# Attention and two gated projections on one core: the transfers of SP's and GpSimd's queues take the list's order

## The chip, the core and the metric

The kernel runs on 1 core of one Trainium2 chip. Times are device microseconds of one execution. Where several executions were timed, their median stands with the lowest and the highest. One further execution was taken with the hardware profiler; all rows below are from that one.

## What is computed

Inputs are q, k, v of 4 batches, 8 heads, 576 positions, 64 values a head. The reference, cut to what matters (the attention has a coarse part on means of four positions and a banded part; two gated blocks follow):

```python
q_d = q.reshape(B, H, Sd, factor, D).mean(axis=3)          # k_d, v_d likewise; factor = 4
out_up = np.repeat(sm_attn(q_d, k_d, v_d), factor, axis=2)
mask = np.abs(pos[:, None] - pos[None, :]) < factor
scores = np.where(mask, scale * np.matmul(q, k.transpose(0, 1, 3, 2)), -1e9)
out_local = np.matmul(softmax(scores), v)
x = (out_up + out_local).transpose(0, 2, 1, 3).reshape(B, S, H * D)
h = np.maximum(x @ w_in, 0.0)                               # 512 -> 1024
x = (h * sigmoid(conv3(h))) @ w_out                         # 1024 -> 512
out = (sigmoid(causal_conv5(x)) * (x @ w_val)) @ w_out2     # 512 -> 512
```

The weights arrive as 64-bit floats and are made into 32-bit ones on the chip.

## The kernel before

**Steps.** Attention runs in 16 steps: step s is batch s // 4 and a pair of heads. A step transposes K and Q on PE (tpk, tpq), evacuates them on ScalarE (kT, qT), forms banded scores in blocks of 24 queries by 32 keys (sl) and coarse scores (sd), and multiplies the exponentials with V: avl and avm read the V windows of the step (a tile `ldw`), avd reads the sums of four V rows (a tile `vd`, or `vs` from step 4 on). The blocks a0, a1, ... are the products with w_in (tile `pa`, two blocks a group of 128 columns), b0, b1, ... those with w_out (`pb`), cc and d those of the second gated block (`pc`, `pd`).

**Loads.** On SP's queue: Lk and Lq (`load`, two transfers each from step 4 on) fetch K and Q of a step; Lw (`load_vw`) fetches the V windows of a step in twelve small transfers; Ls (`Weights.load`) fetches one of 16 weight stages of 512 KB, 0 to 7 of w_in and 8 to 15 of w_out; Lz and O are late weights and stores. On GpSimd's queue: Qv (`sum_v`) sums V rows for two steps with four transfers into one tile, of which the last three add to what is there and so wait for the one before; Ql (the last piece of `Weights.pieces`) adds a stage into the low half of the weights, `win` or `wout`.

**A weight job n.** Ls brings it, ab (ScalarE) and cv (VectorE) make 32-bit floats, hi and lo (ScalarE) write the high part and its negative, Ql adds the value to the latter. Four tags of stage buffers are used in turn, so that ab10 uses the place that job 2 leaves when Ql2 has landed. Block a(2f) and a(2f+1) need Ql f; b blocks of column group e need Ql(8 + 2e) and Ql(9 + 2e). p0 (ScalarE, first tap of the second convolution) writes a tile in the place of stages 3, 7, 11 and 14, and so waits for Ql14.

**What sets the order.** A list, `ORDER` (lines 852 to 917), names every operation. The loop at its end runs them in that order, each inside `ordered(F[name], ALL)`: whatever the operation issues on an engine of `ALL` is put behind the last instruction recorded for that engine. Recorded are the instructions that go through `mm` (PE) or a `Noted` object (`vec`, `act`, `pool`). Before, the list binds PE, VectorE and ScalarE:

```python
        with ExitStack() as st:
            for e in engines:
                if e in last:
                    st.enter_context(tc.issue_after(last[e].ins))
            fn()
...
    ALL = ("pe", "vec", "act")
```

The transfers of both queues are called as `nc.sync.dma_start` and `nc.gpsimd.dma_start`, are not recorded, and their place on their queue is the one that the scheduler finds, which may be ahead of the operations beside them in the list.

Of the kernel before, what the change touches and what calls it, by code (L numbers as in the profile page):

```python
# [45 lines left out]
def kernel(  # L46
# [13 lines left out]
    nc = tc.nc  # L60
# [21 lines left out]
    PW = 512  # L82
# [79 lines left out]
    class Weights:  # L162
# [3 lines left out]
            self.jobs = jobs  # L166
            self.stage = stage

        def load(self, n, queue=nc.sync):
            dst, src, r0, nr, c0 = self.jobs[n]  # L170
            wide = PW // nr
            rows = src[r0 * 128 : (r0 + nr) * 128]
            t, w = self.stage(n)
            if src.dtype == F32:
                queue.dma_start(
                    out=w.rearrange("p (r n) -> p r n", r=nr),
                    in_=rows.rearrange("(r p) n -> p r n", p=128)[:, :, c0 : c0 + wide],
                )
            else:
                queue.dma_start(  # L180
                    out=t.rearrange("p (r n) -> p r n", r=nr),
                    in_=rows.bitcast(I32).rearrange("(r p) n -> p r n", p=128)[
                        :, :, 2 * c0 : 2 * (c0 + wide)
                    ],
                )

        def pieces(self, n):
            dst, src, r0, nr, c0 = self.jobs[n]
            plain = src.dtype == F32
            t, w = self.stage(n)  # L190

            def to():
                return [d[:, c0 // 128, r0 : r0 + nr].rearrange("p r n -> p (r n)") for d in dst]

            words = t.rearrange("p (n t) -> p n t", t=2)
            return (
                lambda: plain or sign_off(act, w, words),
                lambda: plain or to_f32(vec, w, words),
                lambda: act.activation(out=to()[0], in_=w, func=AF.Copy),
                lambda: act.activation(out=to()[1], in_=to()[0].bitcast(F32), func=AF.Copy, scale=-1.0),  # L200
                lambda: nc.gpsimd.dma_start(out=to()[1].bitcast(F32), in_=w, accum_op=ALU.add),
            )

    actx = ExitStack()
# [6 lines left out]
    def load(src, tag, b, hp):  # L211

        if b == 0:
            slot = f"hg{'hi' if tag == 'ldk' else 'lo'}{hp}"
            if hp < 2:
                t = mp.tile([QT, 2, NT, D], F32, tag=slot, name=tag)
                nc.sync.dma_start(
                    out=t.rearrange("p e t d -> p e (t d)"),
                    in_=src[b, 2 * hp : 2 * hp + 2].rearrange("h (p t) d -> p h (t d)", p=QT),
                )  # L220
            else:
                t = mp.tile([QT, NT, 2, D], F32, tag=slot, name=tag)
                for e in range(2):
                    nc.sync.dma_start(  # L224
                        out=t[:, :, e, :], in_=src[b, 2 * hp + e].rearrange("(p t) d -> p t d", p=QT)
                    )
        else:
            t = ap.tile([QT, NT, 2, D], F32, tag=tag, name=tag, bufs=1)
            for e in range(2):
                nc.sync.dma_start(  # L230
                    out=t[:, :, e, :], in_=src[b, 2 * hp + e].rearrange("(t p) d -> p t d", p=QT)
                )
        T[tag, b, hp] = t

    def sum_v(s):

        b, hp = where(s)
        t = ap.tile([HD, 2, 2, 2, D], F32, tag="vs", name="vs")
        rows = v[b, 2 * hp : 2 * hp + 4].rearrange("h (s p r) d -> p (h s) r d", s=2, r=4)
        for r in range(4):  # L240
            nc.gpsimd.dma_start(  # L241
                out=t.rearrange("p t h s d -> p (t h s) d"),
                in_=rows[:, :, r],
                **({"accum_op": ALU.add} if r else {}),
            )
        for i in range(2):
            T["vd", s + i] = t[:, i]

    def load_v_first(part):

        if part == 0:
            first["v"] = keep.tile([HD, H, 2, 4, D], F32, tag="wout1", name="ldv")
        n = H // 2
        t = first["v"][:, part * n : part * n + n]
        nc.sync.dma_start(
            out=t.rearrange("p h s r d -> p (h s) (r d)"),
            in_=v[0, part * n : part * n + n].rearrange("h (s p r) d -> p (h s) (r d)", s=2, r=4),
        )
        for hp in range(part * HP // 2, (part + 1) * HP // 2):
            T["ldv", 0, hp] = first["v"][:, 2 * hp : 2 * hp + 2]  # L260
# [20 lines left out]
    def load_vw(b, hp):  # L281
        vw = ap.tile([128, NG, 2, D], F32, tag="ldw", name="ldw", bufs=1)
        for c in range(4):
            j = c * NG
            while j < (c + 1) * NG:
                n = 1 if j in (0, NB - 1) else min((c + 1) * NG, NB - 1) - j
                g = j - c * NG
                for e in range(2):
                    nc.sync.dma_start(
                        out=vw[KB * c : KB * c + KB, g : g + n, e],  # L290
                        in_=windows(b, 2 * hp + e, key_start(j), n),
                    )
                j += n
        T["ldw", b, hp] = vw
# [257 lines left out]
    E = {}  # L552
# [100 lines left out]
    def late_load(i):  # L653
        if "ep" not in E:
            actx.close()
            end_open()
        src, j = LATE[i]
        rows = src[j * 128 : j * 128 + 128]
        raw = E["ep"].tile([128, 2 * PW], I32, tag="stage", name="stage", bufs=3)
        if src.dtype == F32:  # L660
            nc.sync.dma_start(out=raw[:, :PW], in_=rows.bitcast(I32))
        else:
            nc.sync.dma_start(out=raw, in_=rows.bitcast(I32))
        E["raw", i] = raw

    def late_sign(i):
# [99 lines left out]
        act.activation(out=E["o", i], in_=E["pd", i], func=AF.Copy, scale=0.5)  # L766

    def store(i):
        nc.sync.dma_start(out=oflat[i * 128 : i * 128 + 128, :], in_=E["o", i])

    make_identity(nc, ident)
    for hp in range(3):
        load(k, "ldk", 0, hp)
        load(q, "ldq", 0, hp)
    load_v_first(0)
    load_vw_first(nc.sync, (0, 1, 2))
    pool.memset(mask, 0.0)
    m3 = mask[:, : NG * KB].rearrange("p (g k) -> p g k", k=KB)
    spans = [(c, 0, NG, 4) for c in range(4)]
# [275 lines left out]
```

## Time and profile before

| | us |
|---|---|
| three timed executions, median (lowest to highest) | 481.89 (480.61 to 482.44) |
| the profiled execution, own time | 479.92 |
| its span, first to last instruction | 478.0 |
| PE busy in the span | 427.8 (89%) |
| VectorE busy | 347.5 (73%) |
| ScalarE busy | 282.9 (59%) |
| GpSimd busy | 54.2 (11%) |

The span is cut into stretches below, because the engine that sets the pace differs between them. A busy PE is not PE at its peak: ends of matmuls are modelled. A line of a timeline starts with the time from the span's start and the duration; what stands in brackets at its end is the idle time of the engine just before it and what ended that.

### The profile page before, as it was taken

To read this page: it belongs to the slowest core of one execution; us is meant where nothing else is said; L and a number is where in the kernel's file an instruction comes from. 1 tells how busy PE (TensorE), PEld (TensorE's weight loads), DVE (VectorE), ACT (ScalarE), POOL (GpSimd) and SP (SyncE) were. 2 spreads that over 40 slices of the span, in tenths; PEclk is the share of its full clock that TensorE was granted. 3 is DMA by queue.
4 is the path that set the end of the run, shared out by engine and by line. 5 is a ranking of instruction groups with operands and counts; after the bars stand their busy time and mean duration, and the time that the engine had idled before them with its cause. 6 is when DMAs were issued, how large, how long until landed. Compare 5 with 4: busy or idle time off the path is not lost.

```text
span 478.0 us, 13683 instructions
## 1 busy us (share of the span) xinstructions
PE 427.8 (89%) x5873; PEld 396.6 (83%) x5873; DVE 347.5 (73%) x575; ACT 282.9 (59%) x628; POOL 54.2 (11%) x72
## 2 busy tenths in 40 slices
PE   6257078879999799999999999999999999999996
PEld 5236057779999798999999999999999998989985
DVE  3355099898998589998568769789999999932300
ACT  2344198787986386888657668555793554532221
POOL 8213012111222210022120000000000000000000
PEclk9755555679999899999999999999999999999999
DMA  9999568765466952144671211333000001011022
GB/s 188 169 192 224 132 124 212 187 140 134 94 91 129 122 86 52 36 85 54 108 109 32 63 32 34 134 98 124 1 1 0 2 1 66 23 67 45 22 89 88
DMA packets 90102, 42.91 MB, mean 90 GB/s; under 512 B 74198, under 2 KB 84354, under 8 KB 90042
## 3 DMA queue, kind: packets, MB, share of 16 engines
q1 hardware_dynamic: 73050, 33.88, 28.5%
q0 software_dynamic: 16992, 8.16, 13.5%
q8 instruction: 46, 0.75, 0.7%
q14 instruction: 14, 0.11, 0.1%
HBM read 33.08 MB, written 4.72 MB: 79 GB/s over the span
## 4 chain that ended last, share of the span: by engine, by line
PE 63%; DVE 16%; DMA 8%; SPq 7%; issue 4%; ACT 2%; POOL 1%; POOLq 0%; ACTq 0%; DVEq 0%
PE pb L124 18%; PE pa L124 15%; PE pc L124 11%; PE pd L124 11%; DVE stage L134 4%; DVE cv L134 4%; DMA ldq<-in_q_dram 2%; PE avl L124 2%; DMA ldw<-in_v_dram 2%; SPq L270 2%; SPq L224 2%; PE tp L124 2%; PE sl L124 1%; DMA vs<-in_v_dram 1%; DVE el L134 1%
## 5 line engine op out<-in xcount | busy, mean ns | idle before, releaser
L124 PE MATMUL pa<-xhi,win 128*128 128x288 f32 x512 | 99.8, 308 | 0.0
L124 PE MATMUL pb<-hghi,wout 128*128 128x288 f32 x512 | 95.5, 298 | 0.0
L124 PEld LDWEIGHTS pa<-xhi,win 128*128 128x128 f32 x512 | 79.8, 196 | 1.5 <-issue 1.2
L124 PEld LDWEIGHTS pb<-hghi,wout 128*128 128x128 f32 x512 | 76.2, 188 | 1.7 <-issue 1.6
L134 DVE SCALAR_TENSOR_TENSOR cv<-h,cwt,cv 128x576 f32<-128x576 f32 x64 | 52.1, 815 | 11.6 <-ACT cv L134 10.4
L124 PE MATMUL pa<-xlo,win 128*128 128x288 f32 x256 | 56.6, 303 | 0.1
L124 PE MATMUL pb<-hglo,wout 128*128 128x288 f32 x256 | 54.4, 293 | 0.0
L134 DVE SCALAR_TENSOR_TENSOR g<-y,cwt,g 128x576 f32<-128x576 f32 x64 | 51.6, 816 | 2.3 <-ACT g L134 0.9
L124 PE MATMUL pc<-ys,wval 128*128 128x288 f32 x384 | 51.7, 294 | 0.0
L124 PEld LDWEIGHTS pc<-ys,wval 128*128 128x128 f32 x384 | 51.3, 188 | 0.4
L124 PE MATMUL pd<-wout,hghi 128*128 128x512 f32 x144 | 45.3, 395 | 0.0
L241 POOL DMA_DIRECT2D vs<-in_v_dram x24 | 30.8, 1359 | 112.2 <-DMA vs<-in_v_dram 52.0
L124 PEld LDWEIGHTS pa<-xlo,win 128*128 128x128 f32 x256 | 42.8, 196 | 0.3 <-issue 0.3
L124 PEld LDWEIGHTS pb<-hglo,wout 128*128 128x128 f32 x256 | 41.1, 188 | 0.0
L134 ACT ACTIVATE h<-pa 128x576 f32<-128x576 f32 x32 | 20.7, 647 | 23.0 <-PE pa L124 23.0
L124 PEld LDWEIGHTS pd<-wout,hghi 128*128 128x128 f32 x144 | 26.8, 188 | 6.1
L124 PE MATMUL sl<-kT,qT 64*24 64x32 f32 (+1 forms) x1536 | 17.7, 211 | 15.5 <-ACT qT L134 8.6
L124 PEld LDWEIGHTS sl<-kT,qT 64*24 64x24 f32 (+1 forms) x1536 | 15.3, 110 | 18.4 <-ACT qT L134 9.4
L124 PEld LDWEIGHTS avl<-et,ldw 32*64 32x64 f32 x1536 | 26.3, 153 | 4.5 <-issue 2.7
L124 PE MATMUL avl<-et,ldw 32*64 32x24 f32 x1536 | 28.3, 229 | 1.1 <-issue 1.1
L124 PE MATMUL pd<-wout,hglo 128*128 128x512 f32 x72 | 28.5, 395 | 0.0
L134 ACT ACTIVATE cv<-cv 128x576 f32<-128x576 f32 x32 | 21.6, 680 | 11.4 <-DVE cv L134 11.2
(97 smaller groups left out, 710.4 us busy)
## 6 DMA issues: line engine op xcount, KB each, us to landing
stage<-in_moe_w_out_dram SPq DMA_DIRECT2D x12, 512.0 KB, 4.0
out_dram<-o SPq DMA_DIRECT2D x18, 256.0 KB, 2.0
stage<-in_moe_w_in_dram SPq DMA_DIRECT2D x8, 512.0 KB, 5.6
ldk<-in_k_dram SPq DMA_DIRECT2D x28, 144.0 KB, 4.6
ldq<-in_q_dram SPq DMA_DIRECT2D x28, 144.0 KB, 3.9
vs<-in_v_dram POOLq DMA_DIRECT2D x24, 144.0 KB, 5.0
ldw<-in_v_dram SPq DMA_DIRECT2D x48, 48.0 KB, 2.6
win<-stage POOLq DMA_DIRECT2D x8, 256.0 KB, 6.4
```

The lines of the kernel that those rows point to most:

```text
L124: last["pe"] = nc.tensor.matmul(*a, **kw)
L134: last[self.key] = getattr(self.engine, name)(*a, **kw)
L224: nc.sync.dma_start(out=t[:, :, e, :], in_=src[b, 2 * hp + e].rearrange("(p t) d -> p t d", p=QT))
L241: nc.gpsimd.dma_start(out=t.rearrange("p t h s d -> p (t h s) d"), in_=rows[:, :, r], **({"accum_op": ALU.add} if r else {}),)
L270: queue.dma_start(out=vw[KB * c : KB * c + KB, g], in_=v[0, :, k0 : k0 + KB].rearrange("h k d -> k h d"))
```

## The change

SP's engine gets a `Noted` object, `sync`, and all transfers of SP and the sums, shuffles and first windows of GpSimd go through `sync` and `pool`, so that they are recorded. `ALL` gets "sync" and "pool". With that, what each operation of the list issues on either queue is put behind what the list had on that queue before. The list itself, and every operation on PE, VectorE and ScalarE, are as they were.

```diff
@@ -137,7 +137,7 @@
     vec, act = Noted(nc.vector, "vec"), Noted(nc.scalar, "act")
-    pool = Noted(nc.gpsimd, "pool")
+    pool, sync = Noted(nc.gpsimd, "pool"), Noted(nc.sync, "sync")
...
-        def load(self, n, queue=nc.sync):
+        def load(self, n, queue=sync):
...
-                lambda: nc.gpsimd.dma_start(out=to()[1].bitcast(F32), in_=w, accum_op=ALU.add),
+                lambda: pool.dma_start(out=to()[1].bitcast(F32), in_=w, accum_op=ALU.add),
...
         for r in range(4):
-            nc.gpsimd.dma_start(
+            pool.dma_start(
                 out=t.rearrange("p t h s d -> p (t h s) d"),
...
                 for e in range(2):
-                    nc.sync.dma_start(
+                    sync.dma_start(
                         out=vw[KB * c : KB * c + KB, g : g + n, e],
...
     load_v_first(0)
-    load_vw_first(nc.sync, (0, 1, 2))
+    load_vw_first(sync, (0, 1, 2))
...
     def behind_masks():
-        load_vw_first(nc.gpsimd, (3,))
+        load_vw_first(pool, (3,))
...
-    ALL = ("pe", "vec", "act")
+    ALL = ("pe", "vec", "act", "sync", "pool")
```

The other lines of the diff are the same replacement of `nc.sync` by `sync` in `load`, `load_v_first`, `late_load`, `store` and the load of the convolution taps.

**SP's queue, from the load of Q for step 4 on, before.** A transfer's row names the tile it writes and the tensor it reads: `stage` is a weight stage (Ls), `ldk` and `ldq` are K and Q, `ldw` the V windows. The five `ldw` rows are Lw4.

```order
L230 DMA ldq<-in_q_dram 96x6x64 x2
L289 DMA ldw<-in_v_dram 32x64 x2
L289 DMA ldw<-in_v_dram 32x5x64 x2
L289 DMA ldw<-in_v_dram 32x6x64 x4
L289 DMA ldw<-in_v_dram 32x5x64 x2
L289 DMA ldw<-in_v_dram 32x64 x2
L180 DMA stage<-in_moe_w_in_dram 128x4x256 x3
L230 DMA ldq<-in_q_dram 96x6x64 x2
L180 DMA stage<-in_moe_w_in_dram 128x4x256
L230 DMA ldk<-in_k_dram 96x6x64 x2
L180 DMA stage<-in_moe_w_out_dram 128x4x256 x4
L230 DMA ldk<-in_k_dram 96x6x64 x2
```

The same place with the change; all recorded transfers carry the line of `Noted`, 134:

```order
L134 DMA ldq<-in_q_dram 96x6x64 x2
L134 DMA stage<-in_moe_w_in_dram 128x4x256 x3
L134 DMA ldq<-in_q_dram 96x6x64 x2
L134 DMA stage<-in_moe_w_in_dram 128x4x256
L134 DMA ldk<-in_k_dram 96x6x64 x2
L134 DMA stage<-in_moe_w_out_dram 128x4x256 x3
L134 DMA ldw<-in_v_dram 32x64 x2
L134 DMA ldw<-in_v_dram 32x5x64 x2
L134 DMA ldw<-in_v_dram 32x6x64 x4
L134 DMA ldw<-in_v_dram 32x5x64 x2
L134 DMA ldw<-in_v_dram 32x64 x2
L134 DMA ldk<-in_k_dram 96x6x64 x2
```

Lw4 moved from in front of Ls4, Ls5 and Ls6 (the first `stage` row) to behind Ls9, Ls8 and Ls11; the fourth w_out stage, Ls10, now follows Lk6. The rest of SP's queue is in the same order before and after.

**GpSimd's queue, from the middle of the masks' making on, before.** `vs` is a transfer of Qv, `win` and `wout` are Ql, `ldw` the last windows of the first batch, the memsets clear padding.

```order
L241 DMA vs<-in_v_dram 72x8x64 x2
L134 AFFINE_SELECT mask<-mask 32x192
L134 AFFINE_SELECT mask<-mask 32x160
L134 AFFINE_SELECT mask<-mask 32x32 x2
L270 DMA ldw<-in_v_dram 32x8x64 x6
L800 MEMSET h_78 128x578
L800 MEMSET h_79 128x578
L801 MEMSET qT 128x8
L241 DMA vs<-in_v_dram 72x8x64 x4
L201 DMA win_76<-stage 128x512
L241 DMA vs<-in_v_dram 72x8x64 x2
L201 DMA win_76<-stage 128x512 x7
```

The same place with the change:

```order
L134 DMA ldw<-in_v_dram 32x8x64 x6
L800 MEMSET h_78 128x578
L800 MEMSET h_79 128x578
L801 MEMSET qT 128x8
L134 DMA win_76<-stage 128x512 x2
L134 DMA vs<-in_v_dram 72x8x64 x8
L134 DMA win_76<-stage 128x512 x4
L134 DMA wout_1209<-stage 128x512
L134 DMA win_76<-stage 128x512 x2
L134 DMA wout_1209<-stage 128x512 x3
```

The eight transfers of Qv4 and Qv6 stood among the masks, before Ql0 and behind it; now they stand together behind Ql0 and Ql1 and before Ql5, Ql2, Ql3 and Ql4.

**GpSimd's queue further on, in batch 0's second half, before** (Qv8, Qv10 among the last Ql of w_out):

```order
L241 DMA vs<-in_v_dram 72x8x64
L201 DMA wout_1209<-stage 128x512
L241 DMA vs<-in_v_dram 72x8x64 x3
L636 MEMSET y_2144 128x4x4
L201 DMA wout_1209<-stage 128x512
L241 DMA vs<-in_v_dram 72x8x64
L201 DMA wout_1209<-stage 128x512
L241 DMA vs<-in_v_dram 72x8x64 x3
L201 DMA wout_1209<-stage 128x512
```

With the change:

```order
L134 DMA vs<-in_v_dram 72x8x64 x4
L134 DMA wout_1209<-stage 128x512 x2
L636 MEMSET y_2144 128x4x4
L134 DMA vs<-in_v_dram 72x8x64 x4
L134 DMA wout_1209<-stage 128x512 x2
```

Ql15 and Ql11 now both follow Qv8, and Ql14 and Ql13 both follow Qv10; before, Ql15 stood behind Qv8's first transfer and Ql13 behind Qv10's first.

## Rows read from the trace of the kernel before

**Rows 1.** Table by stretch: us, busy us of five engines, granted clock, DMA share, GB/s.
```profile
36.00:49.00 13.00, 9.22 (x263) 8.04 (x243) 6.63 (x13) 5.56 (x14) 3.78 (x3) 0.50 1.21 220
49.00:55.50 6.50, 0.78 (x55) 0.63 (x55) 0.00 (x0) 0.00 (x0) 0.00 (x0) 0.50 0.25 49
60.00:150.00 90.00, 80.56 (x1425) 72.42 (x1425) 85.26 (x160) 76.36 (x188) 16.69 (x18) 0.78 0.65 137
186.00:478.00 292.00, 287.68 (x3286) 271.02 (x3286) 212.16 (x328) 166.42 (x338) 10.35 (x11) 1.00 0.22 55
```

**Rows 2.** Timeline of ScalarE, the first read of Ls4's words (ab4).
```profile
58.08 0.66 ACT L134 ACTIVATE stage<-stage 128x512 f32<-128x512 f32 x1 [16.02 <-DMA stage<-in_moe_w_in_dram]
```

**Rows 3.** Chain that ended last, in order of time: start, us, what.
```profile
38.89 11.82 DMA ldq<-in_q_dram
...
54.29 3.76 DMA stage<-in_moe_w_in_dram
```

**Rows 4.** Timeline of SP's queue: Lw4, and Ls9, Ls8, Ls11, Ls10.
```profile
43.48 10.68 SPq L289 DMA_DIRECT2D ldw<-in_v_dram  x12
...
74.33 12.91 SPq L180 DMA_DIRECT2D stage<-in_moe_w_out_dram  x4
```

**Rows 5.** Timelines of PE (avl4) and ScalarE (ab10, p0).
```profile
111.09 0.89 PE L124 MATMUL avl<-et,ldw 32*64 32x24 f32 x48
...
105.38 0.68 ACT L134 ACTIVATE stage<-stage 128x512 f32<-128x512 f32 x1
...
173.81 1.44 ACT L134 ACTIVATE g<-y,cwt 128x576 f32<-128x576 f32 x2 [1.75 <-DMA wout<-stage]
```

**Rows 6.** Timeline of GpSimd: Qv4 and Qv6 begin, Ql1, Qv8, Qv10's first and last, Ql14.
```profile
4.37 1.82 POOL L241 DMA_DIRECT2D vs<-in_v_dram  x2
...
62.11 0.91 POOL L201 DMA_DIRECT2D win<-stage  x1 [21.00 <-ACT win L134]
...
130.74 1.43 POOL L241 DMA_DIRECT2D vs<-in_v_dram  x1 [2.75 <-DMA vs<-in_v_dram]
...
150.97 0.88 POOL L241 DMA_DIRECT2D vs<-in_v_dram  x1 [3.37 <-PE avd L124]
...
167.61 1.38 POOL L241 DMA_DIRECT2D vs<-in_v_dram  x1 [3.36 <-DMA vs<-in_v_dram]
168.55 1.39 POOL L201 DMA_DIRECT2D wout<-stage  x1
```

**Rows 7.** Tile vs: readers on PE, issues on GpSimd (ns min/median/max, first start), landing.
```profile
L124 PE MATMUL avd<-etd,vs x96: 286/286/338, 99.5 to 294.6; 72*64 72x144 f32 x96
L241 POOL DMA_DIRECT2D vs<-in_v_dram x24: 845/1379/2148, 4.4 to 246.3; - x24
...
DMA to landing us min/median/max: 3.5/5.0/11.3
```

**Rows 8.** DMA queues, 0 to 24 us, then 24 to 50: packets, MB, share; landing.
```profile
q1 hardware_dynamic: 7511, 3.26, 76.8%
q0 software_dynamic: 1888, 0.99, 32.1%
...
q1 hardware_dynamic: 9474, 4.38, 78.5%
q0 software_dynamic: 3280, 0.86, 33.3%
...
vs<-in_v_dram POOLq DMA_DIRECT2D x4, 144.0 KB, 8.7
```

**Rows 9.** Timelines of PE (sl3, a4) and VectorE (mxl3).
```profile
49.85 0.78 PE L124 MATMUL sl<-kT,qT 64*24 64x32 f32 x55 [3.54 <-issue]
...
104.43 0.83 PE L124 MATMUL pa<-xhi,win 128*128 128x288 f32 x2
...
62.66 0.54 DVE L134 TENSOR_REDUCE mxl<-sl 128x12 f32<-128x384 f32 x1
```

**Rows 10.** Tile win: landing of its transfers (Ql0 to Ql7).
```profile
DMA to landing us min/median/max: 3.6/6.4/7.7
```

More of the change, by code (lines that the diff above doesn't have):

```diff
@@ L223, in load @@
                 for e in range(2):
-                    nc.sync.dma_start(
+                    sync.dma_start(
                         out=t[:, :, e, :], in_=src[b, 2 * hp + e].rearrange("(p t) d -> p t d", p=QT)
@@ L229, in load @@
             for e in range(2):
-                nc.sync.dma_start(
+                sync.dma_start(
                     out=t[:, :, e, :], in_=src[b, 2 * hp + e].rearrange("(t p) d -> p t d", p=QT)
@@ L254, in load_v_first @@
         t = first["v"][:, part * n : part * n + n]
-        nc.sync.dma_start(
+        sync.dma_start(
             out=t.rearrange("p h s r d -> p (h s) (r d)"),
@@ L288, in load_vw @@
                 for e in range(2):
-                    nc.sync.dma_start(
+                    sync.dma_start(
                         out=vw[KB * c : KB * c + KB, g : g + n, e],
@@ L660, in late_load @@
         if src.dtype == F32:
-            nc.sync.dma_start(out=raw[:, :PW], in_=rows.bitcast(I32))
+            sync.dma_start(out=raw[:, :PW], in_=rows.bitcast(I32))
         else:
-            nc.sync.dma_start(out=raw, in_=rows.bitcast(I32))
+            sync.dma_start(out=raw, in_=rows.bitcast(I32))
         E["raw", i] = raw
@@ L768, in store @@
     def store(i):
-        nc.sync.dma_start(out=oflat[i * 128 : i * 128 + 128, :], in_=E["o", i])
+        sync.dma_start(out=oflat[i * 128 : i * 128 + 128, :], in_=E["o", i])
     make_identity(nc, ident)
@@ L836 @@
         if src.dtype == F32:
-            nc.sync.dma_start(out=cwf[o : o + m], in_=src.rearrange("t (f p) -> (t f) p", p=128))
+            sync.dma_start(out=cwf[o : o + m], in_=src.rearrange("t (f p) -> (t f) p", p=128))
         else:
-            nc.sync.dma_start(
+            sync.dma_start(
                 out=cw[o : o + m, :256], in_=src.bitcast(I32).rearrange("t (f p) -> (t f) p", p=256)
```

## The prediction

> **What bounds the kernel now.** I read three stretches. In the table by stretch the last one, 186 to 478 us, has PE busy 287.7 of 292.0 us at a granted clock of 1.00 with the DMA engines at 0.22 [rows 1]: TensorE sets the end there, and a transfer can only move the point at which that stretch begins. In 60 to 150 us VectorE is busy 85.3 of 90 us and the DMA engines 0.65 [rows 1]: VectorE's list sets the pace, with little slack to swallow a shift. The stretch before is different: to 49 us the DMA engines are full (1.21 where transfers of two queues overlap), then from 49.0 to 55.5 us they stand at 0.25, VectorE and ScalarE do nothing and PE 0.8 us [rows 1]. So something is issued late, not moved slowly. ScalarE names it: at 58.08 it ends an idle time of 16.02 us that a weight stage's landing ended [rows 2]. It is ab4, the first read of what Ls4 brings, and all behind it on ScalarE waits. The chain goes back from there: Ls4 took 3.76 us from its issue at 54.29, and before it stands 11.82 us for the landing of a Q load issued at 38.89, at 50.7 [rows 3]. What fills SP's queue between is Lw4: twelve V-window transfers, 43.48 to 54.16 [rows 4], for a step whose values matmuls PE reads first at 111.09 [rows 5]. Beside it, GpSimd's queue carries the sums Qv4 and Qv6, eight transfers from 4.37 on [rows 6], of which PE reads the first at 99.5 [rows 7].
>
> **The change, part by part.** On PE, VectorE and ScalarE no instruction moves. Three things move on the two queues.
>
> 1. *Lw4 goes behind the third w_out stage (Ls11), and Ls4 moves up twelve places.* Ls4 now stands at SP's turn of 43.48 instead of 54.29 [rows 3, 4], and whatever makes that turn earlier makes Ls4 earlier.
>
> 2. *Qv4 and Qv6 leave the first 50 us.* From the queue table: in 0 to 24 us the software queue takes 32.1 of 108.9 parts of the engines' time, 29.5% of some 22 busy us, 6.5 us; four Qv transfers of 144 KB are 0.59 of its 0.99 MB, so 3.9 us. In 24 to 50 us it is 33.3 of 111.8, of some 25 busy us 7.4 us; the other four are 0.59 of 0.86 MB, so 5.1 us [rows 8]. Together 9.0 us less work in front of Ls4. Seven of Lw4's transfers went into that stretch too, 7/12 of 288 KB, 0.8 us at the 220 GB/s of rows 1. The queue that drained at 49 us drains at about 39; Ls4 behind it lands after at most its 3.76 us [rows 3], at 43. **Gain: 58.05 - 43 = 15 us.**
>    Is there something next in line? ScalarE's earlier work ended at 42.06 (58.08 less 16.02) [rows 2], so it does not take more than 1 us away even if it comes no earlier. PE's score matmuls for step 3 end at 50.63, and VectorE reads them at 62.66 [rows 9], 47.7 after a gain of 15: they have to come 3 us earlier. They follow the same early loads, whose first 24 us alone lose 3.9 us, so I let them. If they did not, the gain would be 12.
>    Bounds: if the hardware queue loses nothing to the sums, Ls4 still cannot land before the Q load in front of it, at 50.7: a gain of 7.3. If Ls4 lands with the queue's end instead of after it, it is up to 18.
>
> 3. *The sums now stand between Ql1 and the other seven Ql transfers of w_in on GpSimd's queue, and each waits there.* Qv4 and Qv6 are chains of four transfers that add to one tile, so six of the eight issues wait for the landing before. In the trace such a chain ran undisturbed from 150.97 to 167.61, three steps of 5.55 us [rows 6]. Working with times 15 us earlier: Ql1 at 62.11 becomes 47.1, and its issue takes 0.9. Qv4 starts at 48.0, its last issue is at 64.6 and takes 1.4; Qv6 goes from 66.0 to 82.6, over at 84.0; Ql5 0.9 in front, Ql2 at 84.9 [rows 6]. With the median of 6.4 us to landing [rows 10] Ql2 is there at 91.3. Its first reader, the matmul of block a4 at 104.43 [rows 9], stands at 89.4. **Loss: 1.9 us.** a4 is on the path, as ScalarE, VectorE and the next PE blocks hang on it. Ql3 and Ql4 follow at 0.9 us each and are read later. The bounds of a step: 3.5 and 11.3 us, the shortest and longest landing of such a transfer [rows 7]; at 3.5 Ql2 is 12 us earlier and costs nothing, at 11.3 it lands at 125.8. I take 5.55, since those steps ran beside weight loads and a busy VectorE, as these will. Qv4 itself has landed near 71, and its reader at 99.5 [rows 7] becomes 84.5.
>
>    Other costs are nothing, with their cover. Lw4's issue now stands between Ls11 and Ls10. SP spends 12.91 us from 74.33 on four stages there, waiting for buffers [rows 4]; 15 us earlier it is done at 72.2, and with all of Lw4's 10.68 us behind it Ls10 lands by 87. Its reader ab10 at 105.38 [rows 5] becomes 90.4, Lw4's at 111.09 becomes 96.1. Were that cover gone, it would be at most the 10.68. Further on, Qv8 passes Ql15, whose blocks are the last of four in w_out. Qv10 passes Ql13; Ql14 keeps its place behind Qv10's last transfer (167.61, 168.55 [rows 6]), and p0 on ScalarE, which ended its wait for that landing at 173.81 [rows 5], moves with it. Ql13 follows Ql14 by one issue, 0.9 us, and its reader b10 stands well behind p0 in the list.
>
> **Sum:** 15 - 1.9 = 13.1 us. The profiled execution took 479.9 us (span 478.0), so 466.8, with a span near 464.9. The three timed runs have a median of 481.9, 2.0 above it; against them **468.8 us**. Half a per cent, 2.4 us, is about what a measurement of this kernel can tell from no change.
>
> **A rule that speaks against it.** What the rows show: GpSimd's issue of such a transfer takes 0.85 to 2.15 us, median 1.38 [rows 7], and 1.43 at 130.74 [rows 6], within the stretch in which VectorE is 95% busy [rows 1]. So I give no issue more than 1.4.
> The Trainium skill, "SBUF — State Buffer", section "SBUF: two separate sides", says that a DMA issued from GpSimd gets no descriptors while VectorE runs a two-port performance-mode operation, and the change takes eight such issues from a half-idle VectorE to a full one. By the pair in its next section (some 620 ns alone, 3100 ns beside a VectorE copy) I estimate 5.5 us more for each of eight issues, 44 us, and the sum would be a kernel some 31 us slower; the trace's 1.43 us does not agree.
>
> **The rivals.**
> - *Only Lw4 counts* (the sums ran in gaps of the hardware queue). For: queue shares add to over 100%, so time is counted twice. Against: that queue stood full beside them to 49 us. Gain 7.3, the same 1.9 lost: 476.5 us. 0.13.
> - *The gain is eaten by GpSimd's queue.* With 7.35 to 8.15 us a step Ql2 lands about when a4 ran before: within 0.5% of 481.9. For: it lies between 5.55 and the 8.7 us to landing in 24 to 50 us [rows 8]. Against: it is not near the 5.55. 0.09.
> - *Slower: Qv4 and Qv6 hold Ql2 back past its old due time.* Place: GpSimd's queue before Ql2. It decides from a step of 91.3 + 6x = 104.4, x = 2.2, so 7.75 us. For: the four sums' transfers issued in 24 to 50 us took a median of 8.7 to land [rows 8], and the new stretch has stage loads as well. Against: that stretch was full throughout, the new one has the 0.65 of rows 1. At 8.7 Ql2 lands at 110.2, 5.8 us after a4's old start: 487.7 us. 0.12.
> - *GpSimd's issues are held while VectorE is busy.* With the longest issue of the trace, 2.15 [rows 7], in place of 1.38 for each of the eight, Ql2 comes 6.2 us later and the gain is 6.9: 475.0 us. For: the eight move into VectorE's full stretch. Against: the 1.43 there. 0.03. (It is the skill's rule above, at this trace's own price.)
> - *The list does nothing*, as the scheduler had the same order: excluded by the order of instructions above.
>
> **How the numbers follow.** The forecast, a gain of 8 to 18, has 0.63; its own range is 464 to 474. Lw4's 0.13 and the held issues' 0.03 are faster too: 0.79. Same 0.09, slower 0.12. The range of 8 in 10 goes from the gain's upper bound, 464, over Lw4's case to the near half of no change, 481.5; outside lie the slower case, the other half of no change and a little below 464.
>
> **What would show it.** Right: ScalarE's wait for the stage's landing falls from 16.02 to about 5 us and ends near 43; in 0 to 40 us the software queue has only the six V-window transfers and Ql0; Qv4's four issues begin near 48; PE's a4 starts at 89 to 93 us; the stretch of full PE begins near 173 and is 292 us long as before. Wrong: ab4 after 50 (the hardware queue was not held by the sums); a gap on PE or ScalarE that a w_in transfer of GpSimd's queue ends, over 8 us, near 90 to 110; a last stretch longer than 292.

## The result, and the profile after

Four timed executions of the change have a median of 474.04 us (473.54 to 475.43), four of before beside them 481.25 (479.56 to 482.44): a ratio of 0.986, 95% interval 0.982 to 0.990. In the profiled executions the span went from 478.0 to 471.8 us. The change is faster by 7.2 us, inside the range of the prediction and on the right side, but by little more than half of the 13.1 us forecast. It lies just below the gain of 8 to 18 us that the prediction gave 0.63, and by the number alone nearer to the rivals at 475.0 and 476.5 us; only the traces tell which account holds. Two profiles below (experiments 2 and 4) are of executions over 1.5% slower than the fastest of their kernel, and from these only waits, landings and distances between neighbouring events are read.

The table by stretch after the change, with the columns of [rows 1]:

```profile
36.00:49.00 13.00, 6.40 (x206) 4.96 (x202) 5.34 (x13) 5.19 (x18) 0.43 (x1) 0.50 0.68 179
49.00:55.50 6.50, 4.89 (x70) 3.70 (x76) 6.29 (x13) 5.92 (x17) 1.31 (x2) 0.50 0.65 145
60.00:150.00 90.00, 77.56 (x1450) 70.87 (x1449) 77.55 (x141) 66.29 (x154) 26.16 (x25) 0.85 0.80 147
180.00:471.80 291.80, 287.43 (x3284) 270.73 (x3282) 211.76 (x327) 166.49 (x338) 10.37 (x11) 1.00 0.22 55
```

The empty stretch from 49.0 to 55.5 us is gone: VectorE is now busy for 6.29 of its 6.5 us. The last stretch, cut 6 us earlier here, holds the same work in the same time (PE busy 287.43 of 291.8 us against 287.68 of 292.0), so all of the gain was made before it. New is the middle: VectorE fell from 85.3 to 77.6 busy us in the same 90, with the DMA engines at 0.80 in place of 0.65. It waits there now.

The two DMA queues, first 0 to 24 us, then 24 to 50 (packets, MB, share), which answer to [rows 8]:

```profile
q1 hardware_dynamic: 8389, 3.47, 73.7%
q0 software_dynamic: 192, 0.39, 8.7%
...
q1 hardware_dynamic: 8875, 5.05, 76.7%
q0 software_dynamic: 144, 0.26, 5.5%
```

The software queue fell from 32.1 to 8.7% and from 33.3 to 5.5%. ScalarE's timeline, ab4, ab10 and p0, against [rows 2, 5]:

```profile
44.53 0.66 ACT L134 ACTIVATE stage<-stage 128x512 f32<-128x512 f32 x1 [7.75 <-DMA stage<-in_moe_w_in_dram]
...
94.59 0.67 ACT L134 ACTIVATE stage<-stage 128x512 f32<-128x512 f32 x1 [1.79 <-DMA win<-stage]
...
167.43 1.45 ACT L134 ACTIVATE g<-y,cwt 128x576 f32<-128x576 f32 x2 [2.52 <-DMA wout<-stage]
```

The wait for Ls4 fell from 16.02 to 7.75 us, and ab4 runs 13.55 us earlier. ab10 shows a wait for a w_in transfer that it did not have, and p0's wait for Ql14 grew from 1.75 to 2.52. The chain that ended last goes through these places:

```profile
39.12 5.39 DMA stage<-in_moe_w_in_dram
...
86.61 1.37 POOL vs L134
88.01 6.56 DMA win<-stage
94.61 4.45 PE pa L124 x20
...
103.20 3.26 issue
106.46 4.64 PE pa L124 x33
```

Ls4 is issued at 39.12 and lands 5.39 us later. From 86.61 on the chain is what the prediction feared: Qv6's last issue, then Ql2's landing at 94.57, then block a4. Behind it stands something that was not in the prediction: PE waits 3.26 us for no operand ("issue"), in the middle of block a6. PE's timeline shows both (a4's first step, its second, and a6):

```profile
91.42 0.83 PE L124 MATMUL pa<-xhi,win 128*128 128x288 f32 x2
...
94.61 1.33 PE L124 MATMUL pa<-xhi,win 128*128 128x288 f32 x4 [1.89 <-DMA win<-stage]
...
106.46 0.40 PE L124 MATMUL pa<-xlo,win 128*128 128x288 f32 x1 [3.26 <-issue]
107.23 0.43 PE L124 MATMUL pa<-xlo,win 128*128 128x288 f32 x2
```

The same places before (a4's second step, a6's third and fourth):

```profile
105.54 1.16 PE L124 MATMUL pa<-xhi,win 128*128 128x288 f32 x4
...
113.85 0.80 PE L124 MATMUL pa<-xlo,win 128*128 128x288 f32 x2
...
115.00 0.42 PE L124 MATMUL pa<-xlo,win 128*128 128x288 f32 x2
```

And GpSimd's timeline: Ql1, Qv4's first issue, its last with Qv6's first, Qv6's last, the crowd of eight Ql behind it, and Ql14 with Ql13. The bracket at 86.61 names VectorE, but the transfer before it in the chain had landed only 0.28 us before, at 86.33.

```profile
48.57 0.85 POOL L134 DMA_DIRECT2D win<-stage  x1 [15.15 <-ACT win L134]
49.14 1.17 POOL L134 DMA_DIRECT2D vs<-in_v_dram  x1
...
66.86 2.31 POOL L134 DMA_DIRECT2D vs<-in_v_dram  x2 [3.26 <-DMA vs<-in_v_dram]
...
86.61 1.38 POOL L134 DMA_DIRECT2D vs<-in_v_dram  x1 [6.51 <-DVE el L134]
87.42 4.15 POOL L134 DMA_DIRECT2D win<-stage  x4
89.65 2.80 POOL L134 DMA_DIRECT2D wout<-stage  x1
90.19 4.01 POOL L134 DMA_DIRECT2D win<-stage  x2
...
160.57 2.38 POOL L134 DMA_DIRECT2D wout<-stage  x2
```

The best reading of such a trace is a table of gains: how much earlier than before each of five points of the program is reached. The points are ab4 (58.08 before), a4's second step (105.54), a6's fourth step (115.00), p0 (173.81) and the end of the span (478.0). The other columns are experiments told below, with their numbers.

| us earlier at | change | again (5) | SP alone (1) | Qv6 late (3) | + Qv10 late (6) | + Ls4 first (8) | best (11) |
|---|---|---|---|---|---|---|---|
| ab4 | 13.6 | 13.6 | 4.5 | 14.0 | 12.6 | 15.9 | 14.6 |
| a4, second step | 10.9 | 8.0 | 4.7 | 12.2 | 8.6 | 14.7 | 13.9 |
| a6, fourth step | 7.8 | 2.2 | 4.9 | 13.1 | 8.5 | 13.2 | 12.9 |
| p0 | 6.4 | 2.2 | 4.6 | 11.3 | 11.3 | 17.8 | 18.0 |
| end | 6.2 | 2.1 | 4.4 | 11.2 | 10.7 | 17.5 | 17.6 |

In the first column 2.6 us are lost before a4, 3.2 between a4 and a6, 1.4 between a6 and p0, and next to nothing after that. In the second, the same kernel once more, it is 5.6, 5.8 and nothing.

### The profile page after: what moved, and what is told of

It reads as the page before. It is cut to its first block, busy times and chain, and to the rows that moved or that the text cites. A ratio compares the mean times of both kernels' runs of the same rounds, so it can differ in the third digit from the quotient of the medians.

```text
span 471.8 us, 13676 instructions
## 1 busy us (share of the span) xinstructions
PE 430.3 (91%) x5873; PEld 398.1 (84%) x5873; DVE 347.6 (74%) x575; ACT 282.9 (60%) x628; POOL 54.6 (12%) x72
## 4 chain that ended last, share of the span: by engine, by line
PE 63%; DVE 16%; DMA 8%; SPq 6%; issue 4%; ACT 2%; POOL 1%; ACTq 0%; POOLq 0%; DVEq 0%
PE pa L124 17%; PE pb L124 16%; PE pc L124 11%; PE pd L124 11%; SPq L134 6%; DVE stage L134 4%; DVE cv L134 2%; DMA vs<-in_v_dram 2%; PE avl L124 2%; DMA ldw<-in_v_dram 2%; DVE g L134 2%; PE sl L124 1%; DMA wout<-stage 1%; DMA win<-stage 1%; PE tp L124 1%
## 5 line engine op out<-in xcount | busy, mean ns | idle before, releaser
L134 DVE SCALAR_TENSOR_TENSOR cv<-h,cwt,cv 128x576 f32<-128x576 f32 x64 | 52.1, 815 | 13.9 <-ACT cv L134 12.6
L134 ACT ACTIVATE o<-pd 128x512 f32<-128x512 f32 x18 | 10.6, 596 | 29.8 <-PE pd L124 29.8
L134 ACT ACTIVATE cv<-cv 128x576 f32<-128x576 f32 x32 | 21.6, 679 | 11.3 <-DVE cv L134 11.0
L134 DVE SCALAR_TENSOR_TENSOR gvf<-g,pc 128x576 f32<-128x576 f32 x16 | 11.7, 749 | 19.7 <-PE pc L124 19.6
```

The costliest lines, as they stand in the source:

```text
L134: last[self.key] = getattr(self.engine, name)(*a, **kw)
```

## The experiments

Ratios are to the kernel before on the same chip, with 95% intervals. Each experiment has one trace.

**1. SP's queue alone.** The sums, the Ql and the last windows of the first batch are issued unrecorded, and "pool" leaves the list's engines. All of GpSimd's queue is then as before.

```diff
-    ALL = ("pe", "vec", "act", "sync", "pool")
+    ALL = ("pe", "vec", "act", "sync")
-            pool.dma_start(
+            nc.gpsimd.dma_start(
```

> Only SP's queue takes the list's order; GpSimd's queue is as before (Qv4 and Qv6 among the masks, Ql15 and Ql13 behind the first transfers of Qv8 and Qv10). Theory (both halves are needed for the early Ls4, and each loss sits on GpSimd's queue): the sums still share the DMA engines, so Ls4 lands right behind the Q load at about 51 and ScalarE's ab4 ends its wait at 50 to 52 (58.1 before, 44.5 with the change): 6 to 7.5 us gained there. No sum stands in front of Ql2, so nothing of it is lost near 90, PE's issue stall of 3.26 us does not appear, and Ql14 lands alone: 474 to 476 us. Rival A (the sums cost the hardware queue nothing): ab4 at 45, and without the losses behind it 467 to 469 us. Rival B (Lw4 alone is worth nothing): 480 to 482 us.

Measured: 475.46 us, ratio 0.991 (0.987 to 0.994). ScalarE, ab4:

```profile
53.61 0.66 ACT L134 ACTIVATE stage<-stage 128x512 f32<-128x512 f32 x1 [11.56 <-DMA stage<-in_moe_w_in_dram]
```

It gains 4.5 us at ab4, less than the 6 to 7.5 expected, and keeps them: 4.4 at the end. No wait for Ql2, no stall in a6 over 0.2 us. So both halves of the change are needed for the 13.6 us at ab4, and every loss comes with GpSimd's new order.

**2. GpSimd's queue alone.** All of SP's transfers go back to `nc.sync`.

```diff
-    ALL = ("pe", "vec", "act", "sync", "pool")
+    ALL = ("pe", "vec", "act", "pool")
-                    sync.dma_start(
+                    nc.sync.dma_start(
```

> Only GpSimd's queue takes the list's order; SP's is as before, with Lw4 in front of Ls4. Theory: Lw4's twelve transfers begin where Ls4 begins with the change, at 39.1, and hold it by their 10.7 us of issue less what lay idle: ab4 at 52 to 55, a gain of 3 to 6 there. The sums start behind Ql1 near 49 as with the change, so Ql2 lands near 94.5 and takes little from a gain this small; Ql14 with Ql13 behind it takes 1.6: 477 to 480 us. Rival A (the sums alone make the gain): ab4 near 45 and 473 to 475 us, as with the whole change. Rival B (the sums' new place costs more than it gives): over 482 us.

Measured: ratio 0.998 (0.994 to 1.002), no difference that can be told. ab4 waits until 51.62, which is a gain of 6.5 us, more than the 3 to 6 expected, and PE shows both losses:

```profile
102.64 1.33 PE L124 MATMUL pa<-xhi,win 128*128 128x288 f32 x4 [2.59 <-DMA win<-stage]
...
115.09 0.40 PE L124 MATMUL pa<-xlo,win 128*128 128x288 f32 x1 [2.84 <-issue]
```

The sums' new place buys 6.5 us at ab4, and these two waits, 5.4 us together, spend most of it by a6. Together the halves gain more at ab4 (13.6) than one by one (4.5 and 6.5). With the change Ls4 is issued at 39.12 and lands 5.39 us later. With Lw4 in front of it (experiment 2) it is issued at 47.83; with the sums at their old place (experiment 1) it is issued at 46.96, as SP ends Lq4's issue only at 46.83, and lands 6.63 us later.

**3. Qv6 late.** In the list, from behind avd3 to behind Ql8:

```diff
-        avd3 Qv6 ab7 od3 mxd4
+        avd3 ab7 od3 mxd4
-        mxd5 th0 c1 Ql8 md5
+        mxd5 th0 c1 Ql8 Qv6 md5
```

> The change, with Qv6 moved in the list from behind avd3 to behind Ql8. Theory: Ql5 is issued behind Qv4's last transfer near 68 and Ql2 right behind it, landing before 80, so the waits for it at 94.6 (1.9 us on PE and on ScalarE) go, and the eight accumulates no longer fall into 4 us; if their crowd also makes PE's issue stall of 3.26 us at 106.5, that goes too: 3 to 6.5 us less than the change, 467.5 to 471 us. Rival A (the stall belongs to the place in PE's program, not to the transfers): it stays, 1.5 to 3 us less than the change, 471 to 472.5 us. Rival B (another wait ends at the same time, as VectorE sets the pace there): within 1 us of the change.

Measured: 468.53 us, ratio 0.974 (0.969 to 0.979). GpSimd issues Ql5, Ql2, Ql3 and Ql4 some 20 us earlier:

```profile
67.79 4.38 POOL L134 DMA_DIRECT2D win<-stage  x4
```

and PE has neither wait:

```profile
93.37 0.95 PE L124 MATMUL pa<-xhi,win 128*128 128x288 f32 x4
...
101.17 0.40 PE L124 MATMUL pa<-xlo,win 128*128 128x288 f32 x1 [0.53 <-issue]
```

As the theory had it. 14.0 us at ab4 are 11.2 at the end, so with Qv6 behind them the late a4 goes and the stall goes but for 0.53 us, whichever way the second hangs on the first.

**4. Ql13 early.** Qv10 is cut into its first transfer (Qa10) and the other three (Qb10), with Ql13 between, as before.

```diff
-        Ls14 b5 od7 Lq9 Qv10 xlo6
+        Ls14 b5 od7 Lq9 Qa10 xlo6
-        me7 lo13 rc7
+        me7 lo13 Ql13 Qb10 rc7
```

> The change, with Ql13 issued between Qv10's first transfer and its other three, as before, so that Ql14 stands alone behind the last. Theory (Ql13 beside it makes Ql14's landing 6.8 us in place of 5.2): ScalarE's p0 is 1.6 us earlier, 472 to 473 us. Rival A (Qv10's chain takes Ql13's transfer into its first step instead and ends later by as much): within 0.5 us of the change. Rival B (p0 is not on the path): PE's last stretch begins where it does with the change, no difference though Ql14 lands 1.6 us earlier.

Measured: ratio 0.989 (0.985 to 0.994), nothing gained on the change. Ql14 alone lands in 4.7 us here, against 6.8 in the change with Ql13 beside it; but in the change once more (experiment 5) it landed in 4.8 with Ql13 beside it, so that is not what decides. Qv10's chain takes 19.2 us from its first issue to Ql14's, against 17.3 in the change, 16.2 in experiment 5 and 17.6 before. The time fits rival A; that Ql13 costs as much in front as beside is not shown.

**5. The change once more**, on another chip.

> The change itself once more, on the chip of this group's other kernels, as their yardstick. Both theories: 473 to 476 us, PE's issue stall of about 3 us behind the crowd of eight accumulates again, at the same matmul of block a6 or a7.

Measured: 474.22 us (472.65 to 477.66), ratio 0.988 (0.984 to 0.992). Its profiled execution is the longest of the five, and shows where they differ:

```profile
97.59 1.33 PE L124 MATMUL pa<-xhi,win 128*128 128x288 f32 x4 [5.19 <-DMA win<-stage]
...
111.48 0.61 PE L124 MATMUL pa<-xlo,win 128*128 128x288 f32 x1 [4.39 <-issue]
```

With ab4 at 44.49, as in the first trace, a4 waits 5.19 us for Ql2 instead of 1.89 and a6 stalls 4.39 instead of 3.26. In these two traces the gain at ab4 is the same; what is lost behind it differs by several us. After the longer stall PE also runs slower: from 111.4 to 116.2 us its granted clock is 0.50 (the level of 1.2 GHz), and in the first trace, from 106.4 to 112.0, it is 1.00 (2.4 GHz).

**6. Qv10 late as well**, on top of experiment 3.

```diff
-        Ls14 b5 od7 Lq9 Qv10 xlo6
+        Ls14 b5 od7 Lq9 xlo6
-        md8 mul8 xd8 a20 tr8 qd9 h9 Ql14 ga8 a21 w9 Ql13 p0
+        md8 mul8 xd8 a20 tr8 qd9 h9 Ql14 ga8 a21 w9 Ql13 Qv10 p0
```

> The kernel with Qv6 behind Ql8, and Qv10 moved in the list to behind Ql13. Theory (p0 waits for Ql14, and Ql14 only for Qv10's four chained transfers in front of it on GpSimd's queue): lo14 ends at 154.3, so Ql14 is issued there in place of 157.5 and has landed before p0 is due at 159.6; p0's wait of 2.84 us goes and the time is 2 to 3 us less than with Qv6 behind Ql8 alone: 465 to 467 us. Rival A (p0 is not on the path): p0 earlier, time within 1 us of 468.5. Rival B (Qv10's sums then arrive late at avd10): over 469 us.

Measured: 465.58 us, ratio 0.970 (0.966 to 0.973). p0's wait fell from 2.84 us (experiment 3) to 0.19:

```profile
162.52 1.45 ACT L134 ACTIVATE g<-y,cwt 128x576 f32<-128x576 f32 x2 [0.19 <-DMA wout<-stage]
```

So what p0 waited for was Qv10's four chained transfers in front of Ql14. The interval overlaps that of experiment 3; the wait is what shows it. This execution, again the longest of its five, has a new wait on PE: step 6's transposes, at 94.01, wait 5.92 us for Lq6.

**7. Qv6's last transfer alone late.** Qc6 is Qv6's first three transfers, Qd6 the fourth.

```diff
-        avd3 Qv6 ab7 od3 mxd4
+        avd3 Qc6 ab7 od3 mxd4
-        lo8 Ql3 mxl5 a3 hi9 Ls12 Ql4 rc4
+        lo8 Ql3 mxl5 a3 hi9 Ls12 Ql4 Qd6 rc4
```

> The change, with the last of Qv6's four transfers moved from in front of Ql5, Ql2, Ql3 and Ql4 to behind them, so that these four are issued some 6.5 us earlier, near 80, and Ql9, Ql6, Ql7 and Ql8 where they were, near 88. Theory: Ql2 lands near 86, a4's wait of 1.9 us goes; two crowds of four about 7 us apart leave the DMA engines less full near 105, and PE's issue stall shrinks to under 1.5 us: 469.5 to 471.5 us. Rival A (the stall follows the late a4, 11.8 us behind it in each run that has it, not the crowd): the wait goes and the stall with it, to nothing. Rival B (the stall belongs to that matmul's place in time and to the weight stages loaded there): 3 us of stall stays, 471.5 to 473 us.

Measured: 470.96 us, ratio 0.979 (0.976 to 0.983). a4's wait and a6's stall are gone altogether, but PE stands before step 6's transposes:

```profile
94.82 1.19 PE L124 MATMUL tp<-ident,ldq 96*128 96x96 f32 x6 [8.18 <-DMA ldq<-in_q_dram]
```

SP's queue says why: Lw4, then Lk6, Ls10 and Lq6.

```profile
69.81 9.77 SPq L134 DMA_DIRECT2D ldw<-in_v_dram  x12
79.68 1.14 SPq L134 DMA_DIRECT2D ldk<-in_k_dram  x2
80.94 0.43 SPq L134 DMA_DIRECT2D stage<-in_moe_w_out_dram  x1
81.49 1.48 SPq L134 DMA_DIRECT2D ldq<-in_q_dram  x2
```

Lw4's issue, which the change moved out of Ls4's way, now stands before Lq6. That is at most a part of it: in the change Lq6 was issued behind the same Lw4 at 80.02, only 1.5 us earlier, and the transposes ran at 88.59 without a wait for it. Here it has not landed before 94.8. From its issue to there GpSimd's queue takes 69.5% of the DMA engines' time, and in the change, from 80.0 to 88.5, it takes 20.9%: the four early Ql, issued from 80.54 on, and Lq6 now fall together.

**8. Ls4 in front of K and Q of step 4**, on top of experiment 6.

```diff
-    load(k, "ldk", 1, 0)
-    load(q, "ldq", 1, 0)
-        mxd1 rc1 ab0 mul1 tpk2 tr1 md1 xd1 cv0 tpq2 kT2 qT2 kd2 Ls4 hi0
+        mxd1 rc1 ab0 mul1 tpk2 tr1 md1 xd1 cv0 tpq2 kT2 qT2 kd2 Ls4 Lk4 Lq4 hi0
```

> The kernel with Qv6 behind Ql8 and Qv10 behind Ql13, and the loads of K and Q for step 4 moved to behind Ls4. Theory (to 44 us the hardware queue is full and Ls4 waits its turn): Ls4 lands 3 to 5 us earlier, ab4 at 39 to 41 in place of 44.1, and the time falls by 2 to 5 us: 461 to 465 us. Rival A (Ls5 and Ls6 take over the bound): ab4 earlier, ab5 not, time within 1 us of the kernel without this move. Rival B (the transposes of step 4's Q, near 57, wait for its load): slower than without the move.

Measured: 462.83 us, ratio 0.963 (0.959 to 0.966), as the theory had it, though ab4 is at 42.17 and not at 39 to 41: Ls4 is issued at 30.47, and its words are read 11.7 us later.

**9. Lw4 behind Lq6**, on top of experiment 8.

```diff
-        scd4 sl4 Lw4 xo3
+        scd4 sl4 xo3
-        kd5 etc4 Lk6 xl4 cv8 tpq5 Ls10 a1 qT5 Lq6 qd5
+        kd5 etc4 Lk6 xl4 cv8 tpq5 Ls10 a1 qT5 Lq6 Lw4 qd5
```

> The kernel with Qv6 and Qv10 late and Ls4 in front of K and Q of step 4, and Lw4 moved in the list from in front of Lk6, Ls10 and Lq6 to behind Lq6. Theory (Lw4's 11.5 us of issue on SP, which the change moved out of Ls4's way, now hold Lq6, whose landing ends a wait of 3.0 us of PE at 87.9): Lq6 is issued when its buffer comes free, near 77 in place of 80.8, the wait goes, and the time falls by 1 to 3 us: 460 to 462 us. Rival A (Lq6 is late for the DMA engines' sake, which are full from 84 on, and not for SP's): the wait stays over 2 us and the time within 1 us of 462.8. Rival B (Lw4 is now late itself): PE's avl4, at 96.4, ends a wait for V windows, 463 us or more.

Measured: 462.86 us, ratio 0.960 (0.956 to 0.965): no gain to be seen over experiment 8. The wait for Lq6 did go, as the theory said, and the time did not:

```profile
85.88 0.71 PE L124 MATMUL tp<-ident,ldq 96*128 96x96 f32 x6 [0.71 <-ACT od L134]
...
88.97 0.52 PE L124 MATMUL pa<-xhi,win 128*128 128x288 f32 x2
...
99.45 0.42 PE L124 MATMUL pa<-xlo,win 128*128 128x288 f32 x2 [3.00 <-issue]
```

a6's stall is back at 3.00 us, and here nothing made a4 late and no eight Ql came at once: neither the crowd nor a late a4 is needed for it. The stall is not all, though: a6's fourth step is still 1.6 us earlier than in experiment 8, p0 0.7 later. What took the rest between the two was not traced.

**10. Ql2 late, no crowd**, on top of the change: Qv6's first two transfers (Qc6), five Ql, its last two (Qd6), and then Ql2.

```diff
-        avd3 Qv6 ab7 od3 mxd4
+        avd3 Qc6 ab7 od3 mxd4
-        hi6 sub4 lo6 xlo1
+        hi6 sub4 lo6 Ql5 Ql3 Ql4 Ql7 Ql6 Qd6 Ql2 xlo1
-        sml4 Ql5 w0 cv9 me4 Ql2 a2
-        lo8 Ql3 mxl5 a3 hi9 Ls12 Ql4 rc4 lo9 mul4 tr4 Ql9 sd5 sub5 h1 c0 xl5 Ql6 avd4 w1 Ql7 od4
+        sml4 w0 cv9 me4 a2
+        lo8 mxl5 a3 hi9 Ls12 rc4 lo9 mul4 tr4 Ql9 sd5 sub5 h1 c0 xl5 avd4 w1 od4
```

> The change, with Ql5, Ql3, Ql4, Ql7 and Ql6 between Qv6's second and third transfer (near 75 to 79), and only Ql2, Ql9 and Ql8 behind its fourth: a4 still waits for Ql2 as in the change, but no eight accumulates come at once. Theory (PE's issue stall comes of the crowd): a4 waits 2 to 5 us for Ql2 near 95, and the stall of 3.3 to 4.4 us at the matmul of block a6 or a7 some 12 us later is under 1 us: 470 to 472 us. Rival (the stall follows the late a4): it is 2.8 us or more again, 473 to 476 us.

Measured: 473.95 us, ratio 0.982 (0.976 to 0.988); a stall of 1.09 us, between the two expectations. By itself it does not decide: PE had waited 8.41 us for Lq6 first, and only 0.88 more for Ql2.

**11. Qv6 in the gap.** On top of experiment 9, Ql6, Ql7 and Qv6 move to directly behind Ql4, where GpSimd's queue stood idle.

```diff
-        Ql4 rc4 lo9 mul4 tr4 Ql9 sd5 sub5 h1 c0 xl5 Ql6 avd4 w1 Ql7 od4
-        mxd5 th0 c1 Ql8 Qv6 md5
+        Ql4 Ql6 Ql7 Qv6 rc4 lo9 mul4 tr4 Ql9 sd5 sub5 h1 c0 xl5 avd4 w1 od4
+        mxd5 th0 c1 Ql8 md5
```

> The kernel with Lw4 behind Lq6, and Ql6, Ql7 and Qv6 in the list directly behind Ql4, ahead of Ql9 and Ql8: GpSimd's queue stood idle there from 72 to 83. Theory (PE's issue stall, 3.0 us at 99.5, is a packet of the instruction queue that comes 7.0 us after a4's start, because the DMA engines are full): Qv6's transfers leave 86 to 106 us in part, Ql9 and Ql8 come near 100, the packet comes 5 to 6 us after a4's start and the stall falls to 1 to 2 us: 460 to 462 us. Rival A (the packet takes 7 us whatever the engines carry, and PE at full clock outruns it): 3 us of stall, 462 to 464 us. Rival B (Qv6 beside Lw4, Lk6, Ls10 and Lq6 makes Lq6 late again): a wait of over 3 us at tpq6, 463 us or more.

Measured: 461.37 us (461.03 to 463.35), ratio 0.957 (0.953 to 0.962), the lowest of the kernels that compute everything: 4.3% under the kernel before, where the change has 1.2 to 1.4%. The intervals of experiments 8 and 9 overlap it. a6 stalls 1.98 us, as the theory had it, but the packet (of PE's instructions, see the next section) comes 8.2 us after a4's start and not 5 to 6.

**12. Less to move.** Experiment 9 without Ql6 to Ql9 and without three of Qv6's transfers.

```diff
-        for r in range(4):
+        for r in range(1 if s == 6 else 4):
-        tr4 Ql9 sd5 sub5 h1 c0 xl5 Ql6 avd4 w1 Ql7 od4
-        mxd5 th0 c1 Ql8 Qv6 md5
+        tr4 sd5 sub5 h1 c0 xl5 avd4 w1 od4
+        mxd5 th0 c1 Qv6 md5
```

> The kernel with Lw4 behind Lq6, leaving out four accumulates (Ql6, Ql7, Ql8 and Ql9) and three of Qv6's four transfers, 1.0 MB and 0.44 MB that fall between 84 and 107 us; the low halves and that sum are then not complete. Theory (full DMA engines make the instruction packet late): it comes under 5.5 us after a4's start and PE's issue stall of 3.0 us falls below 1 us; waits for weight stages and K and Q shrink as well: 457 to 461 us. Rival (PE at full clock outruns the packet, whatever the engines carry): 6.5 to 7.5 us after a4's start and 2.5 to 3 us of stall.

Measured: 459.31 us, ratio 0.954 (0.950 to 0.958). The stall fell to 0.48 us, as the theory said. The packet, though, came 7.4 us after a4's start, as late as in experiment 9 (7.5). Both are true, because a4's start is the wrong place to count from, as the start of step 6's scores shows, in experiment 9 and here:

```profile
92.56 1.00 PE L124 MATMUL sl<-kT,qT 64*24 64x32 f32 x96
...
93.78 1.00 PE L124 MATMUL sl<-kT,qT 64*24 64x32 f32 x96
...
98.10 0.43 PE L124 MATMUL pa<-xlo,win 128*128 128x288 f32 x2 [0.48 <-issue]
```

From there PE reaches the place of the stall after 3.9 us in both kernels, and the packet comes after 3.9 us in experiment 9 and after 1.6 here. So the shorter stall is the earlier packet, as the theory had it. Before the scores a4 itself differs: its matmuls run at 0.52 us a pair there and 0.83 here, at a granted clock of 1.00 and 0.55. From the scores to the packet the two data queues take 120% of the DMA engines' time in experiment 9 (overlaps count twice) and 85% here, which fits the theory, from one trace each.

## Why the prediction was right, and why by half

The cause and the first loss were as forecast. That the time still fell inside the range is partly luck: the range was wide enough for the case in which only Lw4 counts, and losses that the sum did not have happened not to use it up.

**Ls4 earlier: right.** Forecast 15 us (bounds 7.3 to 18), measured 13.55. The cause holds: the queue drains earlier without the sums, and experiments 1 and 2 show that neither half does it alone. Ls4 was issued at 39.12 and took 5.39 us instead of the 3.76 of [rows 3], now right behind Lq4's issue, which SP ended at 38.98. The rival in which only Lw4 counts falls: the sums at their old place leave 4.5 us, not the 7.3 that I took as the least.

**Ql2 behind the sums: right, and low.** Forecast 1.9 us, measured 2.6 in one trace and 5.6 in the other (13.6 less 8.0). The term that was too small is the length of the chain: from Qv4's first issue to Qv6's last I had 34.6 us, six steps of 5.55 and an issue between; measured are 37.5 and 40.4. Qv4 alone took 17.7 us for three steps in the first, 5.9 a step, and 22.4 in the second, 7.5 a step. The 5.55 came from one chain, and not an undisturbed one, as Ql13 was issued inside it at 151.92; a range from several chains would have been the better term. The reader was wrong by one row, which gave some back: a4's first step runs without Ql2, its second (105.54 before) is what waits. The rule of the Trainium skill that I weighed against this ("SBUF — State Buffer", section "SBUF: two separate sides") does not show: with VectorE's list full, GpSimd's longest issue of a sum is 1.47 us. Which of VectorE's operations here run in the mode that the rule is about, no run tells.

**p0: priced at nothing, and not always nothing.** I wrote that Ql14 keeps its place and p0 moves with it. In the first trace 1.4 us are lost between a6 and p0, in the second none. Qv10's chain was no longer than before in either; Ql14 took 6.8 us to land in the first and 4.8 in the second, before 5.2, and Ql13 stood beside it in both traces of the change. So Ql13's new place does not explain it, and what made the 6.8 stays open. Experiment 4 shows that putting Ql13 back gains nothing, experiment 6 that Qv10 itself is what Ql14 should not stand behind.

**a6's stall: a term that the sum lacked**, 3.2 us in the first trace. The kernel before already had it: at 113.85 two matmuls take 0.80 us, in which some 0.4 is a wait, and a row that I used for something else shows it in full, step 3's scores at 49.85 with 3.54 us of "issue" in front [rows 9]. The profile's queue table has a queue of instructions, q8, whose 46 packets carry 0.75 MB in the whole span, 16 KB each; between 80 and 120 us they start 3.4 to 24.4 us apart. The slice of the change from 104.0 to 104.5 us:

```profile
q8 instruction: 1, 0.02, 13.5%
```

That these are PE's is read from their distance: before, from 307 to 455 us, PE starts 242 to 262 matmuls and weight loads from one packet to the next. In every kernel here that stalls at this matmul, PE goes on 2.3 to 3.1 us after such a packet starts. Counted from the start of step 6's scores (96 short matmuls, the row `sl<-kT,qT`, at 99.23 in the change), which stand a little ahead of that matmul in PE's list:

```profile
99.23 1.00 PE L124 MATMUL sl<-kT,qT 64*24 64x32 f32 x96
```

| | scores | packet, us later | PE at a6's place, us later | stall |
|---|---|---|---|---|
| before | 110.16 | 1.8 | 4.0 | 0.10 |
| change | 99.23 | 4.8 | 4.0 | 3.26 |
| again (5) | 103.06 | 6.0 | 4.0 | 4.39 |
| Qv6 late (3) | 96.61 | 1.9 | 4.0 | 0.53 |
| + Qv10 late (6) | 101.56 | 1.9 | 4.0 | 0.20 |
| last sum late (7) | 101.28 | 1.2 | 3.6 | none |
| + Ls4 first (8) | 95.48 | 2.5 | 4.0 | 1.51 |
| Lw4 behind Lq6 (9) | 92.56 | 3.9 | 3.9 | 3.00 |
| no crowd (10) | 104.38 | 2.7 | 4.1 | 1.09 |
| best (11) | 95.44 | 3.3 | 3.8 | 1.98 |
| less to move (12) | 93.78 | 1.6 | 3.9 | 0.48 |

PE's way from the scores to the place takes 3.6 to 4.1 us in all, so the stall goes with the packet. In the change, twice, and in experiments 2 and 4, where eight Ql are begun within some 4 to 5 us, the packet comes 4.6 to 6.0 us after the scores; in all others 1.2 to 3.9. A late a4 is not the cause: in experiments 6 and 7 a4's second step ran at 96.98 and 97.79, later than in the change (94.61), and the stall was 0.20 us and none. The crowd goes with the latest packets, but experiment 9 has 3.9 us without one. How full the engines are does not order them: between scores and packet the two data queues took 111% of their time in the change and 116% in experiment 3, where the packet came after 1.9 us. When the packet is asked for, the trace does not tell, and what holds it up stays open.

The Trainium skill ("Runtime: NRT & Kernel Launch", section "Instruction fetch mechanics") says that each engine's instructions are refilled in blocks of 16 KiB through a DMA queue of their own and that crossing a block is mostly hidden. The packet's size agrees, and at most of the 46 packets it is hidden here too. That the packet is what PE waits for is read from its place in each trace. A reading of why it is not hidden at this place, which no run varied: the scores and the V windows behind them are 144 matmuls with a weight load each, and PE starts these 288 within 1.8 us (99.23 to 100.99 in the change), more than it starts between two packets further on.

The same wait stands in all 14 traces at a third place, step 8's scores, which I had overlooked; it is 0.8 to 3.8 us long, and a packet of q8 starts 2.3 to 2.9 us before its end. Before, and with the change:

```profile
159.79 0.69 PE L124 MATMUL sl<-kT,qT 64*32 64x32 f32 x57 [2.97 <-issue]
...
152.93 0.83 PE L124 MATMUL sl<-kT,qT 64*32 64x32 f32 x57 [3.82 <-issue]
```

The chain that ended last goes through Qv10 and Ql14 there and not through PE, so in these two it cost nothing that the trace shows.

**What I called covered was, but for Lq6.** Lw4 behind Ls11 cost nothing in either trace of the change. Lq6, which I had not counted among the transfers behind Lw4, made PE wait 2.2 to 8.4 us in experiments 4, 6, 7, 8 and 10, all with Lw4 in front of it. In the kernels with Lw4 behind Lq6 (9, 11 and 12) no wait at that place is over 1.5 us. But the change and experiment 3 have Lw4 in front as well and no wait for Lq6, so Lw4's issue is one part and the slow landing, as in experiment 7, another; they were not separated.

## What to carry to other kernels

A gain at the head of a chain is kept only as far as the next thing that was just in time: count the gain at several points down the program, against the trace before, and each drop names the place to look at. Do it with more than one trace, as two of the same kernel lost 7 and 11 us here. Count a wait from a place just ahead of it in the same engine's list: from a4 the packet of experiment 12 looked late, from the scores it was early. Putting a queue into the order of a list moves its waits there as well: a chain of accumulating transfers belongs behind the transfers that someone is waiting for, and here moving two such chains by a few places in the list gained 8.6 us more, where the change by itself gains 6.4 (experiments 6 and 5, medians beside the same kernel before). When one wait goes, ask for what stood hidden under it, in the queue as much as on the engine.

## What was not expected of the hardware

PE's instructions come over the DMA engines that carry the data, one packet of 16 KB at a time (the profile counts q8 in the time of the 16 engines), and PE stood for up to 4.39 us with no operand missing. Lw4's twelve transfers of 288 KB together take SP between 6.33 us (experiment 5) and 11.65 us (experiment 6) of issue. And executions of the change on one chip differ by 5 us (472.65 to 477.66); its two traces have ab4 within 0.04 us of each other and Qv4's second issue within 0.1, and part at Qv4's second step on GpSimd's queue (6.1 us against 8.2).
